# Moving the SBUF tiles of a fused attention and two-MLP kernel to multiples of 2048 bytes

## The chip, the core and the metric

The kernel runs on one core of a Trainium2 chip. The metric is the device time of one execution in microseconds (us); three runs of the kernel before gave 922.79, 922.91 and 923.17 us, a median of 922.91 us.

## What is computed

Attention over q, k, v of shape (4 batches, 8 heads, 576 positions, 64), where heads 0 to 3 see the last 32 positions and heads 4 to 7 every 32nd one; its output, 2304 tokens by 512, goes through two MLPs. In outline:

```
x = attention(q, k, v)                  # (2304, 512)
x = ((x @ w_a) * (x @ w_b)) @ w_out     # d_ff 1536
h = x @ w_in                            # d_ff 2048
out = (h * sigmoid(h)) @ w_out2         # (2304, 512)
```

The weights arrive as 8-byte floats, and the kernel makes 4-byte ones of them itself.

## The kernel before

**Matmuls.** A matmul to be precise to 4 bytes is done in three passes of the fp32r type: an operand is held as a pair (high part, rest), and `PASSES = ((0, 0), (0, 1), (1, 0))` names which part of the weights meets which part of the activations (line 733). Each pass is one LDWEIGHTS (128x128) and one MATMUL with a moving operand of up to 512 columns of 4 bytes, that is 2048 bytes in each partition. TensorE (PE) issues 3864 such matmuls in all, 3240 of them with 512 columns and 624, group 4's, with 256; the rest are the attention's small ones and 48 that keep the clock up.

**Order of the work.** Tokens are cut into four groups of 512 (0 to 3) and one of 256 (4). Batch 0's attention comes first, then groups 0 and 1 go through both MLPs one block at a time (lines 738, 1419 and 1439) with the attention of batches 1 to 3 laid between. After that an event list, sorted by planned time, sets the order for groups 2 to 4. Groups 2 and 3 share the up-projections: a block of both is computed in seven products instead of eight (`Chain`, line 1008 on; its matmul is line 1024), with sums and differences of the blocks as operands. Two chains at a time form a `twin`, whose places between products are filled with down-projections (`down`, line 1085). Twins run twice, once for the first MLP and once for the second; group 4 has its own blocks (lines 738 and 1211).

```
1024  nc.tensor.matmul(self.acc[acc], lhsT=w[:, wi, ...P columns], rhs=x[:, xi, c], ...)
 738  nc.tensor.matmul(ps[:, :T],     lhsT=w[:, wi, c*P:(c+1)*P],  rhs=x[:, xi, c, :T], ...)
1085  nc.tensor.matmul(accs[d],       lhsT=lhsT,                   rhs=rhs, ...)
```

**Operands of the seven products.** `CHAIN_ORDER = (1, 2, 6, 5, 7, 4, 3)`, twelve matmuls for each product of a twin. Products 1, 2 and 7 read A11, A12 and S3, which lie in tiles of the pool `xpool` (in the rows `x`); products 6, 5, 4 and 3 read S2, S1, A22 and S4, which lie in one tile `operands` (bytes 167872 to 200640 of each partition) of a pool `late`, opened on the right side of SBUF when attention has ended; all other operands of these matmuls lie below byte 138112. Their weights lie in tiles `w` (pool `wpool`), as everybody's do: ScalarE (ACT) writes the high part and VectorE (DVE) the rest (lines 730 and 731, 1314 and 1315), from pieces `raw` that a DMA has brought.

**Where tiles lie.** Pools are taken one behind the other from the left end of SBUF, and some from the right end. `xpool` holds activations x and y, `hpool` activations h in pairs, `tpool` and `epool` scratch, `rpool` and `kpool` the raw pieces and the 8-byte words (raw pieces take turns between the two), `spool` the small statistics of the softmax. In a partition, remainders of the start addresses by 2048 are, by the built program's memory plan (and in the last column for the changed program):

| tiles | before | changed |
|---|---|---|
| x, y (`xpool`), h (`hpool`), scratch (`tpool`) | 896 | 0 |
| weights' pairs w (`wpool`), raw pieces of `rpool` | 896 | 0 |
| words and raw pieces of `kpool`, scratch of `epool` | 1280 | 0 |
| `operands`, y2, u2, u3, p1, T of the pool `late` | 1984 | 0 |
| q and k tables, v of the attention | 1856, 960, 1984 | 1920, 1024, 0 |

A row of 512 columns is 2048 bytes, so every moving operand starts with its tile's remainder; a weight block of 128 columns starts 0, 512, 1024 or 1536 bytes behind it.

Of the kernel before, what the change touches and what calls it, by code (L numbers as in the profile page):

```python
# [9 lines left out]
F32 = mybir.dt.float32  # L10
# [8 lines left out]
P = 128  # L19
# [94 lines left out]
def attention_gated_mlp_silu_mlp(  # L114
# [32 lines left out]
    NG = len(groups)  # L147

    cpool = ctx.enter_context(tc.tile_pool(name="cpool", bufs=1))
    xpool = ctx.enter_context(tc.tile_pool(name="xpool", bufs=1))  # L150
    hpool = ctx.enter_context(tc.tile_pool(name="hpool", bufs=4))
    tpool = ctx.enter_context(tc.tile_pool(name="tpool", bufs=2))
    rpool = ctx.enter_context(tc.tile_pool(name="rpool", bufs=5))
    wpool = ctx.enter_context(tc.tile_pool(name="wpool", bufs=5))
    spool = ctx.enter_context(tc.tile_pool(name="spool", bufs=4))
    kpool = ctx.enter_context(tc.tile_pool(name="kpool", bufs=5))
    epool = ctx.enter_context(tc.tile_pool(name="epool", bufs=2))
    dpool = ctx.enter_context(tc.tile_pool(name="dpool", bufs=1, space=bass.MemoryType.DRAM))
    accp = ctx.enter_context(tc.tile_pool(name="accp", bufs=1, space=bass.MemoryType.PSUM))
    ringp = ctx.enter_context(tc.tile_pool(name="ringp", bufs=2, space=bass.MemoryType.PSUM))  # L160
    attp = ctx.enter_context(tc.tile_pool(name="attp", bufs=2, space=bass.MemoryType.PSUM))

    ppool = ctx.enter_context(tc.tile_pool(name="ppool", bufs=1, side="right"))
    ppool.tile([P, 8], F32, name="pad")
    att_ctx = ExitStack()
    lpool = att_ctx.enter_context(tc.tile_pool(name="lpool", bufs=1, side="right"))
    qpool = att_ctx.enter_context(tc.tile_pool(name="qpool", bufs=2, side="right"))
# [1 line left out]

    ident = cpool.tile([P, P], F32, name="ident")  # L170
    ident_b = cpool.tile([P, P], BF16, name="ident_b")
    mask_loc = apool.tile([P, 5, HALF], BF16, name="mask_loc", bufs=1)
    mask_str = apool.tile([P, JR], BF16, name="mask_str", bufs=1)

# [1326 lines left out]
```

## Time and profile before

| | |
|---|---|
| median of three runs | 922.91 us (922.79 to 923.17) |
| the profiled execution | 923.98 us, its span 922.2 us |
| busy: PE, its weight loads, DVE, ACT, POOL (GpSimd) | 98%, 79%, 70%, 58%, 10% of the span |
| granted TensorE clock, mean | 0.994 of 2.4 GHz |
| moved by DMA | 145.32 MB |

The profile counts an instruction as busy from its start to its end. A MATMUL's end lies some 0.16 us behind the start of the next, so how fast matmuls follow each other is read from where runs of them start, or from the chain of waits, which gives each piece only the time that it adds.

### The profile page before, as it was taken

The page shows a single profiled execution, that of the slowest core. Times are in us where ns is not written, and L with a number is a line of the kernel's source. Part 1 is how long each engine was busy: PE and PEld are TensorE (multiplying, and loading weights), DVE is VectorE, ACT ScalarE, POOL GpSimd, SP SyncE. Part 2 cuts the span into 40 slices and gives each one's busy share as a digit, 9 for nine tenths or more (in the row PEclk, how much of TensorE's full clock was granted, in tenths as well). Part 3 has the DMA queues.
Part 4 walks back from the last instruction along what each step waited for, and adds up shares of the span by engine and source line. Part 5 has one row for each costly group of instructions (what it writes and reads, how often), then busy time and mean ns, then how long its engine had stood idle before and what let it go on. Part 6 is the DMA issues. An engine that isn't in the chain of part 4 may idle for free.

```text
span 922.2 us, 16422 instructions
## 1 busy us (share of the span) xinstructions
PE 899.1 (98%) x5914; PEld 731.5 (79%) x5914; DVE 642.9 (70%) x1215; ACT 533.4 (58%) x1270; POOL 92.9 (10%) x162
## 2 busy tenths in 40 slices
PE   9799899999999999999999999999999999999998
PEld 5576677787778878778888888888999888878897
DVE  4577888776767867666677676656687766766475
ACT  4657788665677665564544444355575655554474
POOL 4532222011111010100000000000000000000000
PEclk9799999999999999999999999999999999999999
DMA  9999899898699993423332112233463121235471
GB/s 163 190 296 249 291 274 295 261 243 267 219 264 266 278 272 99 127 80 94 102 113 79 55 53 67 68 103 103 138 183 115 48 90 58 81 83 169 125 204 38
DMA packets 163697, 145.32 MB, mean 158 GB/s; under 512 B 96848, under 2 KB 119952, under 8 KB 163616
## 3 DMA queue, kind: packets, MB, share of 16 engines
q1 hardware_dynamic: 154758, 121.81, 49.6%
q0 software_dynamic: 6912, 21.66, 6.9%
q10 hardware_dynamic: 1946, 0.81, 0.5%
q8 instruction: 46, 0.75, 0.3%
q14 instruction: 35, 0.29, 0.1%
HBM read 121.70 MB, written 22.54 MB: 156 GB/s over the span
## 4 chain that ended last, share of the span: by engine, by line
PE 71%; DVE 9%; DMA 6%; ACT 6%; issue 4%; SPq 3%; POOL 0%; DVEq 0%; ACTq 0%; POOLq 0%
PE ring L738 16%; PE ring L1024 12%; PE att L1024 9%; PE acc L1085 8%; PE acc L1439 6%; PE acc L1211 4%; PE att L1085 4%; PE ring L1085 4%; PE acc L738 3%; PE acc L1419 3%; DMA words<-in_moe_w_b_dram 2%; ACT prs L501 2%; DVE w L731 2%; DVE raw L710 1%; ACT h L748 1%
## 5 line engine op out<-in xcount | busy, mean ns | idle before, releaser
L738 PE MATMUL ring<-x,w 128*128 128x512 f32 (+1 forms) x816 | 166.2, 356 | 4.6 <-DVE w L731 2.9
L738 PEld LDWEIGHTS ring<-x,w 128*128 128x128 f32 x816 | 132.3, 189 | 30.2 <-DVE w L731 7.4
L1315 DVE TENSOR_TENSOR w<-raw,w 128x512 fp32r<-128x512 f32 (+1 forms) x164 | 106.3, 656 | 28.9 <-ACT w L1314 26.2
L1314 ACT CAST w<-raw 128x512 fp32r<-128x512 f32 (+1 forms) x164 | 95.6, 592 | 20.4 <-PE att L1085 11.0
L731 DVE TENSOR_TENSOR w<-raw,w 128x512 fp32r<-128x512 f32 x136 | 93.2, 691 | 4.9 <-ACT w L730 4.4
L1439 PE MATMUL acc<-w,h 128*128 128x512 f32 x384 | 93.4, 392 | 1.3 <-DVE w L731 0.9
L738 PE MATMUL ring<-y,w 128*128 128x512 f32 x384 | 93.5, 392 | 0.3 <-DVE w L731 0.3
L1439 PEld LDWEIGHTS acc<-w,h 128*128 128x128 f32 x384 | 71.3, 188 | 17.7 <-DVE w L731 1.8
L738 PEld LDWEIGHTS ring<-y,w 128*128 128x128 f32 x384 | 71.3, 188 | 15.9 <-DVE w L731 0.7
L730 ACT CAST w<-raw 128x512 fp32r<-128x512 f32 x136 | 82.7, 620 | 2.0 <-PE acc L738 1.1
L1419 PE MATMUL acc<-h,w 128*128 128x512 f32 x288 | 72.5, 397 | 5.6 <-ACT w L730 2.5
L748 ACT CAST h<-h 128x512 fp32r<-128x512 f32 (+1 forms) x48 | 27.2, 567 | 83.0 <-DVE h L1060 40.7
L1419 PEld LDWEIGHTS acc<-h,w 128*128 128x128 f32 x288 | 52.7, 188 | 20.3 <-DVE w L731 4.8
L1024 PE MATMUL ring<-operands,w 128*128 128x512 f32 x240 | 60.6, 395 | 0.0
L749 DVE TENSOR_TENSOR h<-g,h 128x512 fp32r<-128x512 f32 (+1 forms) x64 | 39.9, 624 | 28.9 <-ACT h L748 28.9
L1024 PE MATMUL att<-operands,w 128*128 128x512 f32 x240 | 59.6, 393 | 0.0
L1024 PE MATMUL ring<-x,w 128*128 128x512 f32 x240 | 59.5, 391 | 0.0
L748 ACT CAST h<-g 128x512 fp32r<-128x512 f32 (+1 forms) x64 | 36.3, 567 | 37.7 <-DVE g L1411 30.2
L1130 POOL DMA_DIRECT2D out_dram<-o x16 | 8.7, 545 | 466.1 <-DVE o L1129 465.6
L501 ACT ACTIVATE prs<-sm,nm 128x54 f32<-128x54 f32 (+1 forms) x120 | 39.8, 333 | 25.1 <-DVE nm L486 25.1
L710 DVE SCALAR_TENSOR_TENSOR raw<-e,raw 128x512 int32<-128x512 int32 x68 | 49.0, 721 | 6.9 <-ACT e L687 0.9
L1024 PEld LDWEIGHTS ring<-operands,w 128*128 128x128 f32 x240 | 44.8, 188 | 11.4 <-DVE w L1315 1.3
(202 smaller groups left out, 1554.7 us busy)
## 6 DMA issues: line engine op xcount, KB each, us to landing
raw<-keptp SPq DMA_DIRECT2D x80, 256.0 KB
raw<-kepti SPq DMA_DIRECT2D x64, 256.0 KB
words<-in_moe_w_out_dram SPq DMA_DIRECT2D x28, 512.0 KB
raw<-kepto SPq DMA_DIRECT2D x48, 256.0 KB
raw<-kepta SPq DMA_DIRECT2D x36, 256.0 KB
raw<-keptb SPq DMA_DIRECT2D x36, 256.0 KB
words<-in_moe_w_in_dram SPq DMA_DIRECT2D x16, 512.0 KB
words<-in_moe_w_a_dram SPq DMA_DIRECT2D x12, 512.0 KB
```

Of the source, the lines that this page charges most:

```text
L501: nc.scalar.activation(out=place[s], in_=src[s], func=AF.Exp, bias=st["nm"][:, s:s + 1], scale=1.0, accum_out=su[:, s:s + 1],)
L710: nc.vector.scalar_tensor_tensor(out=z, in0=rebased.pop(c), scalar=3, in1=z, op0=ALU.logical_shift_left, op1=ALU.bitwise_or)
L730: nc.scalar.copy(out=o[:, 0], in_=t)
L731: nc.vector.tensor_tensor(out=o[:, 1], in0=t, in1=o[:, 0].bitcast(F32), op=ALU.subtract)
L738: nc.tensor.matmul(ps[:, :T], lhsT=w[:, wi, c * P:(c + 1) * P], rhs=x[:, xi, c, :T], start=(c == 0 and wi == 0 and xi == 0), stop=(c == CC ...
L748: nc.scalar.copy(out=o[:, 0, :T], in_=t32[:, :T])
L1024: nc.tensor.matmul(self.acc[acc], lhsT=w[:, wi, (2 * part + c) * P:(2 * part + c + 1) * P], rhs=x[:, xi, c], start=(begin and c == 0 and m ...
L1085: nc.tensor.matmul(accs[d], lhsT=lhsT, rhs=rhs, start=(first and wi == 0 and xi == 0), stop=(last and wi == 1))
L1314: nc.scalar.copy(out=o[:, 0, cols], in_=t)
L1315: nc.vector.tensor_tensor(out=o[:, 1, cols], in0=t, in1=o[:, 0, cols].bitcast(F32), op=ALU.subtract)
L1419: nc.tensor.matmul(accs[d], lhsT=w[:, wi, d * P:(d + 1) * P], rhs=h[:, xi], start=(j == 0 and wi == 0 and xi == 0), stop=(j == N1 - 1 and ...
L1439: nc.tensor.matmul(accs[t][:, :DM], lhsT=h[:, xi, t * P:(t + 1) * P], rhs=w[:, wi, :], start=(j == 0 and wi == 0 and xi == 0), stop=(j == ...
```

## The change

Two pads and one move. The unused tile that pads the right side grows from 8 to 504 floats; a new pool `lead` of 288 floats is put between the constants and `xpool`; the pool `spool` is opened behind `epool`. No computation, buffer count, transfer or order is edited: on each of the five queues the changed program has the same instructions in the same order with the same waits, and only addresses differ.

```diff
     cpool = ctx.enter_context(tc.tile_pool(name="cpool", bufs=1))
+    lead = ctx.enter_context(tc.tile_pool(name="lead", bufs=1))
     xpool = ctx.enter_context(tc.tile_pool(name="xpool", bufs=1))
...
     wpool = ctx.enter_context(tc.tile_pool(name="wpool", bufs=5))
-    spool = ctx.enter_context(tc.tile_pool(name="spool", bufs=4))
     kpool = ctx.enter_context(tc.tile_pool(name="kpool", bufs=5))
     epool = ctx.enter_context(tc.tile_pool(name="epool", bufs=2))
+    spool = ctx.enter_context(tc.tile_pool(name="spool", bufs=4))
...
     ppool = ctx.enter_context(tc.tile_pool(name="ppool", bufs=1, side="right"))
-    ppool.tile([P, 8], F32, name="pad")
+    ppool.tile([P, 504], F32, name="pad")
...
     ident_b = cpool.tile([P, P], BF16, name="ident_b")
+    lead.tile([P, 288], F32, name="lead")
```

## Rows read from the trace of the kernel before

**Rows 1.** The page's second part: busy tenths in 40 slices of the span.
```profile
PE   9799899999999999999999999999999999999998
DVE  4577888776767867666677676656687766766475
PEclk9799999999999999999999999999999999999999
DMA  9999899898699993423332112233463121235471
```
**Rows 2.** Stretches of the span: length, busy time of each engine (instructions), clock, DMA.
```profile
core 0: us, PE busy (x) PEld busy (x) DVE busy (x) ACT busy (x) POOL busy (x), PEclk, DMA share, GB/s
50.00:100.00 50.00, 46.27 (x385) 35.09 (x384) 37.68 (x80) 33.93 (x89) 15.18 (x25) 1.00 1.06 287
...
420.00:475.00 55.00, 55.00 (x244) 45.53 (x244) 39.63 (x67) 27.55 (x50) 0.05 (x1) 1.00 0.35 97
```
**Rows 3.** Chain of waits, a quiet stretch: start us, us added, engine and line, instructions.
```profile
424.51 2.72 PE ring L738 x12
427.23 2.72 PE acc L1439 x12
...
465.31 8.16 PE acc L1439 x36
```
**Rows 4.** Chain of waits, a stretch of the first MLP's twins.
```profile
489.95 2.75 PE att L1024 x12
492.70 2.77 PE ring L1024 x12
495.47 2.72 PE att L1024 x12
498.19 2.76 PE ring L1024 x12
500.95 2.75 PE att L1024 x12
```
**Rows 5.** Timeline of PE, the same stretch: start us, us, line, names, shapes, instructions.
```profile
489.79 2.91 PE L1024 MATMUL att<-operands,w 128*128 128x512 f32 x12
492.54 2.93 PE L1024 MATMUL ring<-x,w 128*128 128x512 f32 x12
495.31 2.88 PE L1024 MATMUL att<-x,w 128*128 128x512 f32 x12
498.03 2.93 PE L1024 MATMUL ring<-operands,w 128*128 128x512 f32 x12
500.79 2.91 PE L1024 MATMUL att<-operands,w 128*128 128x512 f32 x12
```
**Rows 6.** Stretches: the first MLP's twins, the second MLP's; columns as in rows 2.
```profile
473.31:612.05 138.74, 138.74 (x607) 113.76 (x606) 96.18 (x171) 57.56 (x109) 2.20 (x4) 1.00 0.24 73
...
707.77:821.05 113.28, 113.28 (x491) 91.62 (x490) 80.03 (x141) 60.30 (x116) 0.00 (x0) 1.00 0.23 71
```
**Rows 7.** Chain of waits, the second MLP's twins.
```profile
739.59 1.39 PE ring L1024 x6
740.98 0.70 PE acc L1085 x3
741.68 1.65 PE ring L1024 x6
```
**Rows 8.** Who waited for whom, 700 to 830 us: total us, times, longest.
```profile
PEld ring L1024 <- DVE w L1315: 1.3, 3, 0.4
```
**Rows 9.** Groups by shape, line 1024: instructions, busy us, mean ns, idle before.
```profile
L1024 PE MATMUL ring<-operands,w 128*128 128x512 f32 x240 | 60.6, 395 | 0.0
L1024 PE MATMUL att<-operands,w 128*128 128x512 f32 x240 | 59.6, 393 | 0.0
```
**Rows 10.** Groups by shape, ACT and DVE, splits of weights from two places.
```profile
L1314 ACT CAST w<-raw 128x512 fp32r<-128x512 f32 x144 | 88.6, 618 | 20.0 <-PE att L1085 11.0 <-ACT w L1314 5.3 <-PE ring L1024 1.1
L1314 ACT CAST w<-T 128x512 fp32r<-128x512 f32 x40 | 24.8, 619 | 17.7 <-DVE T L1324 16.9 <-PE acc L1439 0.8
...
L1315 DVE TENSOR_TENSOR w<-raw,w 128x512 fp32r<-128x512 f32 x144 | 98.7, 688 | 27.1 <-ACT w L1314 24.4
L1315 DVE TENSOR_TENSOR w<-T,w 128x512 fp32r<-128x512 f32 x40 | 27.0, 685 | 0.2
```
**Rows 11.** Stretches of 3.2 us that each hold one raw load; columns as in rows 2.
```profile
533.90:537.10 3.20, 3.20 (x16) 2.62 (x15) 1.67 (x3) 1.72 (x3) 0.00 (x0) 1.00 0.29 82
558.60:561.80 3.20, 3.20 (x16) 2.62 (x15) 1.65 (x3) 1.72 (x3) 0.00 (x0) 1.00 0.34 82
...
747.20:750.40 3.20, 3.20 (x16) 2.61 (x15) 0.73 (x2) 0.59 (x1) 0.00 (x0) 1.00 0.33 82
777.80:781.00 3.20, 3.20 (x16) 2.61 (x15) 0.73 (x2) 0.59 (x1) 0.00 (x0) 1.00 0.31 82
```
**Rows 12.** Chain of waits, first half: waits on kept pieces, runs behind a wait.
```profile
144.61 7.94 DMA raw<-kepta
...
301.90 5.48 DMA kepti<-raw
...
410.66 2.97 PE acc L1439 x12
```

## The prediction

> **What bounds the kernel now.** I read the busy slices first. PE is at nine tenths or more in 37 of 40 slices, at full clock after the second, and neither DVE nor DMA is up with it after the first third [rows 1]. So a change of the time must change how long PE needs, or the few waits it has. The stretches tell where these are: in 50 to 100 us PE is busy for 46.27 of 50.00 us beside a DMA share of 1.06, while from 420 us on it is busy without a hole (55.00 of 55.00) with DMA at a third [rows 2]. The late part can only get faster if matmuls follow each other faster.
>
> How fast they follow is in the chain of waits. In the quiet stretch every 12 fp32r matmuls add 2.72 us, and 36 add 8.16 us, 0.2267 us each [rows 3]. They read y, h and w there, all at remainder 896. In the twins the pieces aren't equal: 2.72 for one run of 12, but 2.75, 2.76 and 2.77 for others [rows 4]. The timeline names what each of them reads. The 2.75 and 2.76 are `operands`; the 2.77 is the first run on `x` behind an `operands` run; the 2.72 is the second run on `x`; the next `operands` run is slow again [rows 5]. The chain's pieces start 0.16 us behind the timeline's, since it counts from the end of what came before. So matmuls that stream `operands` take 2.75/12 = 0.229 us each, and a stream that comes behind them needs about one run to get back to its pace (2.77 - 2.72 = 0.05 us). PE waits for nobody in this (idle before: 0.0, for all 480 of them) [rows 9]. What is different about them is where they lie: `operands` starts at 1984 = 64 mod 128, while everything at 896, weights too, starts on a multiple of 128.
>
> **The change, part by part.**
>
> *x, y, h, w and `tpool` from 896 to 0.* All of them move by the same +1152 bytes, so a weight block and the row that streams through it keep their distance, which was already a multiple of 512. Pace now: 0.2267 us [rows 3]. I take it as unchanged. Bounds: a gain would need their start itself to cost something, a loss that the new one does; no row has an fp32r stream on a multiple of 256, so both are rivals below.
>
> *`operands` from 1984 to 0.* This is the only part that changes the distance of a matmul's two operands (from 64 to 0 mod 128). In the first MLP's twins, 138.74 us hold 606 started matmuls (607 with the one still draining from before) [rows 6]. At 0.2267 us they would take 606 x 0.22667 = 137.36 us; 1.4 us are lost. In the second MLP's twins, 113.28 us hold 489 (491 with two short ones still draining), which need 110.84 us; 2.4 us are lost [rows 6]. But of those, three waits stay: one run of 6 takes 1.65 us where its neighbour takes 1.39 [rows 7], and there are three in which PE's weight load waits for DVE's split (at most 0.4 us each, 1.3 in all, of which 0.26 lands on PE) [rows 7, 8]. 3 x 0.26 = 0.8 us, which leaves 1.6. Together 1.4 + 1.6 = 3.0 us. I take off 0.1 us for four short run-ins behind waits that remain, and say **2.9 us**. The lower end: only `operands`' own runs gain, 480 x (0.2296 - 0.2267) = 1.4 us, and the run-ins stay. The upper end: run-ins behind waits in the first half go as well. The chain has 12 runs of 12 that take 2.94 to 2.98 us behind a wait, the last at 410.66 [rows 12]; if each gave 0.05 to 0.08 us, that adds 0.9 us: 3.9 us.
>
> What is late next? Both stretches are covered by PE alone. DVE is busy for 96 of 139 and 80 of 113 us and ACT for less [rows 6], so 1% less of PE time doesn't make either the bound; their waits are on PE's results and come forward with it. What lies behind the twins, groups of 3 and 4, is PE's too, so I let the whole gain reach the end.
>
> *ACT and DVE.* Their operands move too. A split that reads T (1984) takes 619 ns on ACT and 685 on DVE; one that reads raw (896 or 1280) takes 618 and 688 [rows 10]. Nothing, in either direction; and DVE's is off PE's path but for the 0.8 us above.
>
> *DMA.* Raw pieces of `rpool` move from 896 (128 past a multiple of 256) to 0, those of `kpool` from 1280, a multiple of 256, to 0. Loads into `kpool` (533.90, 558.60) show shares of 0.29 and 0.34, loads into `rpool` (747.20, 777.80) 0.33 and 0.31 [rows 11]: means of 0.315 and 0.32, no difference. I take nothing. The Trainium skill, "DMA: Bandwidth & Descriptors", section "How a descriptor splits into AXI transactions", says that a piece not starting on a multiple of 256 bytes costs an extra transaction; for 2048 bytes at 128 past one that would be 68 beats instead of 64, an estimate from that page. By that rule a load into `rpool` would be some 6% longer, and the rows above don't show it. If 6% were true of stores and loads in the first half, it would shorten the waits on kept pieces in the chain, 7.94 and 5.48 us [rows 12], by 0.8 us, which lies inside the upper end.
>
> *Two pads, the place of `spool`.* No instruction; the statistics that move are 24 bytes long. Zero.
>
> **Sum.** The profiled execution took 923.98 us, 1.07 above the median of the runs. 923.98 - 2.9 = 921.1; the same step from the median gives 922.91 - 2.9 = **920.0 us**. About 0.2% (1.85 us) is what a measurement of this kernel tells from no change.
>
> **The rivals.**
>
> *Nothing happens (17%).* The slow runs may be due to the place of `operands`, at the top of the memory, not to the remainder of its start; it stays there. For it: this is the only operand tile above byte 138112, so place and remainder come together in every row. Against: the five w tiles, which stream in every second run of rows 3, reach from below byte 131072 to above it at one pace [rows 3], and the loss is a small constant for each matmul as from a bad start. Time: 922.9, less or more 0.4. The Trainium skill speaks for this rival: "SBUF — State Buffer", section "Who interferes with whom", gives PE two read ports of its own, one for the stream and one for the weights, that wait on nobody, and "Operand start alignment" asks for no more than the element's size. By these, 1984 is as good as 896 and the sum would be 0; the 2.75 against 2.72 in rows 4 speaks against it, but doesn't say which property of the address is at fault.
>
> *Slower (11%).* The starts at 896, 1408, 1920 and 384 (blocks of a tile at 896) are all 128 past a multiple of 256, and a stream on a multiple of 256 or 2048 was never seen. If that is a bad start for both of PE's reads, as 64 past one is now, all 512-column matmuls but the 480 run as `operands` do: 2760 x 0.0023 (0.2290 - 0.2267) = 6.4 us more, 929.3 us. It decides as soon as 2760 matmuls lose over 2.9/2760 = 1.1 ns each. Against: weight blocks start 0, 512, 1024 and 1536 bytes further and streams 2048, and a run of 12 goes through four blocks and several rows at one pace [rows 3], so steps of 512 and more don't matter; 128 and 256 are all that is left.
>
> *Everything gets faster (5%).* 512 columns in 0.2267 us are 0.0133 more than 512 / 2.4 GHz. If a part of it is due to starts off 256, up to 3240 x 0.0133 = 43 us could go; a tenth of it on top of the 2.9 gives 915.7 us. The Trainium skill, "TensorE: Matmul & The Clock Gate", Part 1, states 215.7 ns for back-to-back matmuls of 512 columns, measured in bf16, which would be 11 ns less than here; no fp32r row shows such a pace at any start.
>
> That the change doesn't do what it says I rule out: the memory plan of the changed program has every tile where the table says, and the instructions and waits are the same.
>
> **How the numbers follow.** Forecast 67%, own range 919.0 to 921.5. Of that I put 7 points at gains under 1.85 us (the lower end, 1.4). Faster: 60 + 5 = 65%. Same: 7 + 17 - 1 = 23%, the 1 being small losses of the second case. Slower: 11 + 1 = 12%. The range takes in the forecast, with 0.6 us beyond its own lower end for what the first half may add, and the case in which nothing happens: 918.4 to 923.3. It leaves out the last two (16%) and some edges.
>
> **What would show it.** Right: in the chain of waits, runs of 12 on `operands` add 2.72 us and the run on `x` behind them too; the first twins' 606 matmuls take about 137.4 us, the second's 489 about 111.7 with the three waits; the quiet stretch stays at 2.72. Wrong: `operands` still at 2.75 (place, not start); or the quiet stretch at 2.75 (the start at 0 is bad); or less waiting in the first half, which I don't count on; or the gain of the twins met by longer waits for DVE's splits.

## The result, and the profile after

| | before | changed |
|---|---|---|
| median of 4 runs | 922.85 us (922.49 to 923.17) | 915.04 us (913.94 to 916.83) |
| ratio | | 0.9917, 95% interval 0.9900 to 0.9934 |
| the profiled execution, its span | 923.98 us, 922.2 us | 914.96 us, 913.1 us |

The change gains 7.8 us where 2.9 were forecast; 915.0 lies below the range. Line numbers in the changed kernel are two higher: L1024 of [rows 4] is L1026, L738 is L740, L1439 is L1441, L1085 is L1087.

The page of the changed kernel, second part, the lines of [rows 1]:

```profile
PE   8799899999999999999999999999999999999998
DVE  4677887876767777666778667755687766766475
PEclk9999999999999999999999999999999999999999
DMA  9999899796899983333332221233463222235461
```

PE is still the busy one. Its clock has no dip in the second slice any more, and DMA falls to a third in the same slice as before, the sixteenth. The stretches of the changed kernel that answer to [rows 2, 6], the twins' ones moved to where they lie now:

```profile
50.00:100.00 50.00, 47.29 (x387) 35.36 (x386) 40.76 (x84) 35.29 (x90) 15.56 (x27) 1.00 0.99 302
...
420.00:475.00 55.00, 55.00 (x245) 45.53 (x244) 41.35 (x70) 28.04 (x51) 2.21 (x4) 1.00 0.38 111
466.55:603.90 137.35, 137.35 (x607) 113.74 (x606) 96.21 (x171) 57.68 (x109) 2.21 (x4) 1.00 0.24 73
699.58:811.97 112.39, 112.13 (x492) 91.32 (x490) 79.99 (x141) 60.39 (x116) 0.00 (x0) 1.00 0.23 71
```

The first twins take 137.35 us where they took 138.74, the second 112.39 where they took 113.28: 1.4 and 0.9 us. The larger part came before: the first twins start at 466.55 instead of 473.31, 6.8 us earlier. 6.8 + 1.4 + 0.9 = 9.1 us, the difference of the two spans. (Of the medians the difference is 7.8; the profiled execution of before lay 1.1 us above its median.) The chain of waits of the changed kernel, the lines of [rows 3, 4, 12] and two waits early on:

```profile
74.02 7.93 DMA words<-in_moe_w_a_dram
85.66 6.67 DMA words<-in_moe_w_out_dram
137.59 5.49 DMA raw<-kepta
...
458.56 8.16 PE acc L1441 x36
...
483.04 2.72 PE att L1026 x12
485.76 2.72 PE ring L1026 x12
488.48 2.72 PE att L1026 x12
491.20 2.72 PE ring L1026 x12
```

and the early waits in the chain of the kernel before:

```profile
75.31 5.55 DMA words<-in_moe_w_b_dram
82.74 8.71 DMA words<-in_moe_w_b_dram
92.65 6.55 DMA words<-in_moe_w_out_dram
```

In the quiet stretch 36 matmuls take 8.16 us as before, but the piece starts at 458.56 instead of 465.31. In the twins all runs of 12 take 2.72. Between 60 and 106 us the chain's long waits for words add up to 14.6 us instead of 20.8; one of 3.6 us for a load of q has come up beside them. What a timeline of PE in the changed kernel shows of two runs in the twins, to set beside [rows 5]:

```profile
482.87 2.88 PE L1026 MATMUL att<-operands,w 128*128 128x512 f32 x12
485.59 2.88 PE L1026 MATMUL ring<-x,w 128*128 128x512 f32 x12
```

and who waited for whom in 695 to 825 us, to set beside [rows 8]:

```profile
PEld ring L1026 <- DVE w L1317: 1.6, 3, 0.5
PEld ring L1026 <- ACT w L1316: 0.8, 3, 0.3
```

Runs on `operands` and on `x` now look alike. But the second MLP's twins wait more for the splits: 1.6 + 0.8 us of weight loads' waits instead of 1.3. The splits themselves take what they took (changed kernel, groups by shape, beside [rows 10]):

```profile
L1316 ACT CAST w<-T 128x512 fp32r<-128x512 f32 x40 | 24.8, 620 | 17.7 <-DVE T L1326 16.9 <-PE acc L1441 0.8
...
L1317 DVE TENSOR_TENSOR w<-T,w 128x512 fp32r<-128x512 f32 x40 | 27.0, 686 | 0.2
```

Where the 6.8 us come from is seen in the first stretches (columns as in [rows 2]). Before:

```profile
0.00:45.00 45.00, 37.89 (x536) 24.09 (x536) 21.28 (x71) 23.68 (x112) 23.41 (x44) 0.90 0.95 178
45.00:90.00 45.00, 42.31 (x424) 31.28 (x423) 33.02 (x72) 28.48 (x73) 12.98 (x22) 0.99 1.05 273
```

Changed:

```profile
0.00:45.00 45.00, 37.42 (x612) 24.21 (x613) 23.89 (x83) 25.83 (x123) 23.43 (x44) 1.00 0.93 195
45.00:90.00 45.00, 43.58 (x374) 33.25 (x373) 34.60 (x74) 31.26 (x78) 14.02 (x23) 1.00 1.00 303
```

DMA engines are busy all the time in both (shares 0.93 to 1.05), but move 195 and 303 GB/s instead of 178 and 273. The 200th fp32r matmul starts at 97.66 us instead of 104.51; the lead is there by then, and later stretches carry it on unchanged. By these rows and the long waits for words I take DMA as what bounds the first 100 us, and it moved more in the same time. Why it did is what the experiments ask.

### The profile page after: what moved, and what is told of

The parts are those of the page before. It is cut to its first block, busy times and chain, and to the rows that moved or that the text cites. A ratio compares the mean times of both kernels' runs of the same rounds, so it can differ in the third digit from the quotient of the medians.

```text
span 913.1 us, 16422 instructions
## 1 busy us (share of the span) xinstructions
PE 891.4 (98%) x5914; PEld 728.4 (80%) x5914; DVE 642.2 (70%) x1215; ACT 533.7 (58%) x1270; POOL 93.3 (10%) x162
## 4 chain that ended last, share of the span: by engine, by line
PE 68%; DVE 13%; ACT 8%; DMA 6%; issue 3%; SPq 2%; DVEq 0%; POOL 0%; ACTq 0%
PE ring L740 17%; PE ring L1026 11%; PE att L1026 7%; PE acc L1441 7%; PE acc L1087 6%; PE acc L1213 4%; PE att L1087 4%; PE ring L1087 4%; PE acc L1421 3%; PE acc L740 3%; ACT prs L503 2%; DVE w L733 2%; DMA words<-in_moe_w_a_dram 2%; DVE w L1317 1%; ACT h L750 1%
## 5 line engine op out<-in xcount | busy, mean ns | idle before, releaser
L740 PE MATMUL ring<-x,w 128*128 128x512 f32 (+1 forms) x816 | 166.2, 356 | 3.7 <-DVE w L733 2.2
L740 PEld LDWEIGHTS ring<-x,w 128*128 128x128 f32 x816 | 132.4, 189 | 29.3 <-DVE w L733 6.5
L1441 PE MATMUL acc<-w,h 128*128 128x512 f32 x384 | 93.5, 393 | 1.3 <-DVE w L733 0.9
L740 PE MATMUL ring<-y,w 128*128 128x512 f32 x384 | 93.5, 392 | 0.3 <-DVE w L733 0.3
L1441 PEld LDWEIGHTS acc<-w,h 128*128 128x128 f32 x384 | 71.3, 188 | 17.8 <-DVE w L733 1.7
L740 PEld LDWEIGHTS ring<-y,w 128*128 128x128 f32 x384 | 71.3, 188 | 15.9 <-DVE w L733 0.7
L1026 PE MATMUL ring<-operands,w 128*128 128x512 f32 x240 | 60.0, 392 | 0.3
L1026 PE MATMUL ring<-x,w 128*128 128x512 f32 x240 | 59.0, 389 | 0.0
L1026 PE MATMUL att<-operands,w 128*128 128x512 f32 x240 | 58.8, 389 | 0.0
L1026 PEld LDWEIGHTS ring<-operands,w 128*128 128x128 f32 x240 | 44.6, 188 | 11.3 <-DVE w L1317 1.6
```

What stands on the lines that cost most here:

```text
L740: nc.tensor.matmul(ps[:, :T], lhsT=w[:, wi, c * P:(c + 1) * P], rhs=x[:, xi, c, :T], start=(c == 0 and wi == 0 and xi == 0), stop=(c == CC ...
L1026: nc.tensor.matmul(self.acc[acc], lhsT=w[:, wi, (2 * part + c) * P:(2 * part + c + 1) * P], rhs=x[:, xi, c], start=(begin and c == 0 and m ...
L1441: nc.tensor.matmul(accs[t][:, :DM], lhsT=h[:, xi, t * P:(t + 1) * P], rhs=w[:, wi, :], start=(j == 0 and wi == 0 and xi == 0), stop=(j == ...
```

## The experiments

Two theories for the 6.8 us. **Clock**: the two dips to half speed, 1.2 GHz (before's profile, 28.9 to 35.8 and 42.6 to 46.0 us), went. **Pieces**: the attention's loads land in tiles that all began 192 past a multiple of 256 (`qld` and `kld`, which the loads of q and k fill, and `vl`, which those of v for heads 0 to 3 fill, at 960, 1472 and 1984), in pieces of 128 bytes (q, k) or 256 bytes (v); in the changed kernel they begin at 1024, 1536 and 0. And two for PE: **start** (each operand must begin on some multiple) and **distance** (from the weights' start to the stream's). `gap` and `lgap` are unused tiles that shift what follows them.

**The two sides apart.** r1_right has the right side of the change alone, r2_left the left alone.

```diff
--- before
+++ r1_right
-    ppool.tile([P, 8], F32, name="pad")
+    ppool.tile([P, 504], F32, name="pad")
--- changed
+++ r2_left
-    ppool.tile([P, 504], F32, name="pad")
+    ppool.tile([P, 8], F32, name="pad")
```

> Only the pad on the right side grows (8 to 504 floats): the chains' operands and the attention's tiles move to where the change puts them, x, h, w, raw and words stay at 896 and 1280. Theory 1 (two starts count: that of operands for PE, 2.9 us, and that of the attention's load tiles for the DMAs of the first half, some 5 us; the left side counts nothing): about 915, as the full change. Theory 2 (the left side's raw pieces, pairs and words shorten the DMAs): about 920, the operands' part alone. Theory 3 (what goes beyond 2.9 us is not a matter of addresses but of the runs): about 920.

> Only the left side moves (the pool lead, spool behind epool; x, h, w, raw, words at 0), operands stay at 1984 and the attention's tiles as before. Theory 1: 922.9, no change. Theory 2: about 918, all that goes beyond the operands' part. Theory 3: 922.9.

r1_right: 918.39 us, ratio 0.9957 (0.9944 to 0.9970). r2_left: 922.20, 0.9994 (0.9985 to 1.0002). So the right side, where `operands` and the attention's tiles lie, gave 4.6 us alone, and yet the first twins got longer in both: 139.12 and 139.27 us from the first start to the last, against 138.52 before and 137.13 in the changed kernel. The two sides don't add up: they work together on PE. Theory 1 had 915 for r1_right and Theory 2 had 918 for r2_left, and both missed; on Theory 3 these two runs don't decide. The chain of r2_left, in the twins:

```profile
487.35 2.80 PE att L1026 x12
490.15 2.74 PE ring L1026 x12
492.89 2.72 PE att L1026 x12
495.62 2.80 PE ring L1026 x12
```

`operands` stayed where it was, at 1984, and is slower than before (2.80 against 2.75), because the left side with w moved. That speaks for distance.

**Operands and the attention's tiles apart.** r3_ops puts `operands` at 0 and leaves the rest, the attention's tiles too; r4_att moves the attention's tiles alone.

```diff
--- before
+++ r3_ops
-    ppool.tile([P, 8], F32, name="pad")
+    ppool.tile([P, 504], F32, name="pad")
+    gpool = att_ctx.enter_context(tc.tile_pool(name="gpool", bufs=1, side="right"))
+    gpool.tile([P, 16], F32, name="gap")
--- before
+++ r4_att
+    gpool = att_ctx.enter_context(tc.tile_pool(name="gpool", bufs=1, side="right"))
+    gpool.tile([P, 496], F32, name="gap")
```

> The right pad of 504 floats, and a second one of 16 floats that goes with the attention's pools: operands at 0, the attention's tiles where they were before (load tiles 192 past a multiple of 256), the left side as before. Theory 1: 920.0, operands' runs of 12 at 2.72 us, and the first half as before (twins begin at about 473 us). Theories 2 and 3: about 920 as well.

> The right pad stays at 8 floats and a second one of 496 goes with the attention's pools: operands at 1984 as before, the attention's tiles where the change puts them (load tiles on multiples of 256), the left side as before. Theory 1: about 918, operands' runs of 12 still at 2.75 us, DMA packets of 128 bytes shorter on the mean and the twins beginning at about 467 instead of 473 us. Theories 2 and 3: 922.9.

r3_ops: 923.95, 1.0006 (0.9993 to 1.0019): no gain, where all three theories had about 920. Its chain in the twins:

```profile
489.65 2.80 PE att L1026 x12
492.45 2.73 PE ring L1026 x12
495.18 2.72 PE att L1026 x12
497.90 2.79 PE ring L1026 x12
```

`operands` at 0 beside w at 896 is slower than at 1984, though both starts are multiples of 128: the criterion of the forecast (multiples of 128, for the starts as for their distance) is not enough. r4_att: 917.64, 0.9946 (0.9934 to 0.9958), 5.3 us gained, where theories 2 and 3 had nothing, with PE's part untouched (its chain):

```profile
458.95 8.16 PE acc L1441 x36
...
483.59 2.75 PE att L1026 x12
486.34 2.77 PE ring L1026 x12
```

and its second stretch:

```profile
45.00:90.00 45.00, 44.43 (x417) 34.22 (x416) 37.33 (x84) 32.67 (x88) 13.63 (x22) 1.00 1.04 302
```

The start of the attention's tiles alone brings 302 GB/s and the quiet stretch at 458.95, nearly as early as in the changed kernel. It did so with a mean granted clock of 0.92 in the first 45 us, near before's 0.90. A kernel of the next part, s1_all896, gains 7.9 us with the clock as low as before's, 0.90 and 0.98 in its first two stretches against 0.90 and 0.99:

```profile
0.00:45.00 45.00, 38.67 (x563) 24.60 (x564) 21.88 (x72) 24.41 (x117) 23.20 (x44) 0.90 0.91 195
45.00:90.00 45.00, 44.44 (x414) 34.10 (x414) 36.38 (x80) 31.61 (x83) 13.76 (x22) 0.98 1.02 288
```

So the clock isn't the cause; the start of the attention's tiles is. Nor is it their place: in r3_ops, and in t4_match below, they lie 2048 bytes lower than before with the same remainders, and the quiet stretch begins at 464.93 and 464.01, with little or nothing of the lead. Whether it is the loads into these tiles, and which, is asked further down.

**Start or distance.** s1_all896 keeps the left side of before and puts `operands` at 896 too; t1_dist256 and s2_dist512 put it at 256 and 512 in the changed kernel. The gap keeps the attention's tiles where the changed kernel has them, by their remainders.

```diff
--- before
+++ s1_all896
-    ppool.tile([P, 8], F32, name="pad")
+    ppool.tile([P, 792], F32, name="pad")
+    gpool = att_ctx.enter_context(tc.tile_pool(name="gpool", bufs=1, side="right"))
+    gpool.tile([P, 224], F32, name="gap")
--- changed
+++ t1_dist256
-    ppool.tile([P, 504], F32, name="pad")
+    ppool.tile([P, 440], F32, name="pad")
...
+    gpool.tile([P, 64], F32, name="gap")
--- changed
+++ s2_dist512
-    ppool.tile([P, 504], F32, name="pad")
+    ppool.tile([P, 376], F32, name="pad")
...
+    gpool.tile([P, 128], F32, name="gap")
```

> The left side as before (x, h, w at 896), the attention's tiles as in the change (load tiles on multiples of 256), and the operands at 896 too, so that their distance to w is 0 as in the change but no start is a multiple of 2048. Theory 4 (the distance of operands and w by 512 sets PE's pace, not the start itself): operands' matmuls at 0.2267 to 0.2270 us, the first MLP's twins in 137.1 us, and about 2.3 us less than with the attention's tiles alone (917.6), so 915.3. Theory 5 (starts on a multiple of 2048, or of 256, are what is needed): operands' matmuls at 0.230 or more, twins 138.5 or more, 917.6 to 918.4.

> The full change with the operands 512 bytes up (512 past a multiple of 2048; a row of theirs now crosses such a multiple), the rest as in the change. Theory 4 by 512: operands' matmuls at 0.2267 to 0.2270 us as in the change, twins 137.1 us, 915. Theory 5, or a distance that counts by 2048: operands' matmuls slow, 0.229 to 0.233 us, twins 138.5 to 139.3, 916.5 to 918.

> The full change with the operands 256 bytes up, so 256 from w's blocks instead of 0. If the distance counts by 256 (or finer, which 128 has ruled out): operands' matmuls at 0.2267 to 0.2270 us, the first MLP's twins 137.1 us, about 915. If it counts by 512: operands' matmuls at 0.229 to 0.233 us, twins 138.5 to 139.3 us, 916.5 to 918.

s1_all896: 915.37, 0.9912 (0.9899 to 0.9925). s2_dist512: 914.35, 0.9911 (0.9897 to 0.9926). t1_dist256: 915.28, 0.9916 (0.9903 to 0.9929). All three gain what the change gains, and their first twins take 137.13 us as its do: Theory 4's numbers, not Theory 5's. The chain of s1_all896:

```profile
484.15 2.72 PE att L1026 x12
486.87 2.72 PE ring L1026 x12
489.59 2.72 PE att L1026 x12
```

and of t1_dist256:

```profile
483.54 2.72 PE att L1028 x12
486.26 2.72 PE ring L1028 x12
```

Not a single start of the matmuls in s1_all896's twins is a multiple of 256, and they have full pace. Put together, by `operands`' start less w's, modulo 256 (mean ns from one start to the next within `operands`' runs, and the chain's time for a run of 12):

| distance mod 256 | kernels | mean ns | 12 matmuls, us |
|---|---|---|---|
| 0 | changed, s1_all896, t1_dist256, s2_dist512 | 226.8 to 226.9 | 2.72 |
| 64 | before, r4_att | 230.4 | 2.75 |
| 128 | r1_right, r3_ops | 232.9 | 2.79 to 2.80 |
| 192 | r2_left | 233.4 | 2.80 |

Distance 0 was seen with both starts at 0 and with both at 128 past a multiple of 256; each other distance with one pair of remainders only (stream 192 and weights 128, 0 and 128, 192 and 0). That other pairs at the same distance take the same time is likely, but not shown.

Once the distance is 0, the left side's move (x, y, h, w and the raw pieces to 0) adds nothing that the medians show: without it 915.37, with it 915.04. About 1 us in the first half isn't excluded: r2_left's first twins got 0.75 us longer, and its median is 0.8 us lower all the same, its quiet stretch (one execution) at 462.62 instead of 465.31.

**Which pieces.** s3_qk moves q's and k's load tiles alone to a multiple of 256, t3_v v's alone. t2_qk128 puts q's and k's at 128 past one in the changed kernel. t4_match is the changed kernel with the attention's tiles back at 192 past: PE's part without the pieces.

```diff
--- before
+++ s3_qk
+    gpool.tile([P, 496], F32, name="gap")
...
+            lpool.tile([P, 16], F32, tag="lgap", name="lgap")
--- before
+++ t3_v
+    gpool.tile([P, 512], F32, name="gap")
...
+            lpool.tile([P, 48], F32, tag="lgap", name="lgap")
--- changed
+++ t2_qk128
+    gpool.tile([P, 32], F32, name="gap")
...
+            lpool.tile([P, 32], F32, tag="lgap", name="lgap")
--- changed
+++ t4_match
+    gpool.tile([P, 16], F32, name="gap")
```

> Only the load tiles of q and k (qld, kld; pieces of 128 bytes) on multiples of 256; v's tiles, the operands and the left side as before. Theory 6 (a DMA piece that crosses a multiple of 256 bytes of SBUF is dearer; both q and k and v count, by the packets' mean times 64512 x 1.9 ns against 23328 x 3.1 ns over 16 engines, 7.7 against 4.5 us): about 60% of the 5.3 us that all of the attention's tiles give, 919.7. If v's tiles do it alone: 923. If q and k do it alone: 917.6.

> Only the load tile of v of heads 0 to 3 (vl; pieces of 256 bytes) on a multiple of 256; q's and k's tiles cross as before, the operands and the left side as before. Theory 6: what the attention's tiles give together (5.3 us) less what q's and k's give alone (3.0): 920.7; packets of 128 bytes stay at 14.5 ns or more on the mean, those of 256 bytes get shorter. If q and k do it alone: 923.

> The full change with q's and k's load tiles at 128 past a multiple of 256 instead of 0 (v's tiles stay on one): no piece of 128 bytes crosses a multiple of 256, but every tile starts off one. Theory 6 (crossing): 915, packets of 128 bytes 13.1 to 13.5 ns on the mean as in the change. Theory 7 (the tile has to start on a multiple of 256): 918, packets of 128 bytes 14.5 ns or more.

> The full change, but the attention's tiles 64 bytes down, where they were before: left side and operands at 0, load tiles crossing multiples of 256. Theory 4 with 6: PE's part alone, twins 137.1 us in the first MLP and 115.3 in the second, the first half nearly as before: 920 to 921, near the 920.0 of the prediction. If the left side's raw pieces matter as well: 918 to 919.

In the table, the gain is against the median of the runs of before on the same chip (922.96, 923.28 or 923.31 us; for the changed kernel 922.85), the ratio is taken over all runs and so isn't the quotient of two medians, the quiet stretch is the start of its piece of 36 in the chain, and the last two columns are means over the trace's records of DMA packets, 64512 of 128 bytes and 23328 of 256:

| kernel | median, us | ratio (interval) | gain, us | quiet stretch, us | 128 B, ns | 256 B, ns |
|---|---|---|---|---|---|---|
| before | | | | 465.31 | 15.2 | 22.3 |
| t4_match | 920.16 | 0.9966 (0.9954 to 0.9979) | 3.2 | 464.01 | 14.3 | 21.8 |
| s3_qk | 920.27 | 0.9962 (0.9948 to 0.9975) | 3.0 | 459.54 | 13.5 | 19.7 |
| t3_v | 919.93 | 0.9970 (0.9961 to 0.9979) | 3.4 | 460.69 | 15.2 | 21.5 |
| r4_att | 917.64 | 0.9946 (0.9934 to 0.9958) | 5.3 | 458.95 | 13.5 | 19.2 |
| t2_qk128 | 915.16 | 0.9912 (0.9899 to 0.9925) | 8.2 | 457.32 | 13.2 | 19.0 |
| changed | 915.04 | 0.9917 (0.9900 to 0.9934) | 7.8 | 458.56 | 13.3 | 19.2 |

The last three columns are of one execution for each kernel, and these scatter: with the attention's tiles at before's remainders the means are 14.3 to 15.2 and 21.3 to 22.3 ns (before, r2_left, r3_ops, t4_match), and the profiled execution of s3_qk took 918.21 us, 2.1 below its median. So the gain of a kernel goes by the medians.

The second stretch of t4_match, against r4_att's 302 GB/s:

```profile
45.00:90.00 45.00, 43.62 (x406) 32.53 (x405) 33.81 (x74) 27.81 (x71) 13.55 (x22) 0.98 1.02 274
```

and its chain:

```profile
464.01 8.16 PE acc L1443 x36
...
480.33 2.72 PE att L1028 x12
```

t4_match has PE's part (2.72 on `operands`) and only 1.3 us of the early lead; r4_att has the lead and not PE's part. 5.3 + 3.2 = 8.5 us against 7.8, within the intervals (each some 1.1 us to either side). q's and k's load tiles alone gain 3.0 us, and t3_v, with `vl`, 3.4. The medians of packets are the same in all (13 and 18 ns): only a tail got shorter, in the changed kernel the 95th percentile of 128-byte packets from 28 to 13 ns and that of 256-byte ones from 46 to 27.

The tail isn't each tile's own. In s3_qk `vl` lies where it did, and the 256-byte packets still fell from 22.3 to 19.7; in t3_v `vl` was moved and they fell by 0.8 only, to 21.5, which is inside the scatter of kernels that left it in place. So q's and k's pieces delay the others beside them, and the shorter 256-byte packets that were expected of t3_v aren't shown. What gained 3.4 us in t3_v these means don't tell. Its second stretch does move as much as r4_att's, with the granted clock in the first as low as before's:

```profile
0.00:45.00 45.00, 38.74 (x564) 24.86 (x565) 21.50 (x72) 24.40 (x117) 23.37 (x44) 0.89 1.02 186
45.00:90.00 45.00, 44.45 (x417) 34.27 (x416) 36.30 (x79) 30.54 (x80) 13.54 (x22) 1.00 1.09 302
```

But t3_v isn't `vl` alone. Its gaps also shift the attention's other tiles, and by 256 these come to the remainders that they have in r4_att: t3_v is r4_att without q's and k's load tiles. (3.0 + 3.4 = 6.4 us against r4_att's 5.3 is within the intervals.) The attention's instructions on these tiles take no less time for it: a matmul on the q and k tables takes a mean of 219 ns (64 columns) in before, t3_v and r4_att alike. Which of the tiles brings the 3.4 us, and by what, stays open.

t2_qk128 loses nothing, so q's and k's tiles needn't begin on a multiple of 256. A piece of 128 bytes in a tile that begins 0 or 128 past such a multiple never lies across one, in a tile at 192 past every second piece does; that fits the rows of q and k, but a rule of multiples of 128 would fit them too, and no run tells these two apart.

**One more tile.** v's small tiles `vs` still begin at 96 in the changed kernel; s4_vs moves them to 0.

```diff
--- changed
+++ s4_vs
+    apool.tile([P, 24], F32, name="vgap", bufs=1)
```

> The full change, and the tile vs (v of heads 4 to 7, pieces of 256 bytes, at 96 past a multiple of 2048 in the change) moved to a multiple of 2048 by a gap of 24 floats. Theory 6: the pieces of vs no longer cross a multiple of 256, packets of 256 bytes get shorter on the mean, and the first half 0.5 to 2 us shorter: 913 to 914.5. If crossing doesn't matter: 915.0.

914.24 us, 0.9900 (0.9887 to 0.9914), the lowest median of all kernels. Packets of 256 bytes got shorter, as expected: 18.5 ns on the mean instead of 19.2, the 95th percentile 18 instead of 27. But the interval overlaps the change's (0.9900 to 0.9934), and the quiet stretch starts no earlier (458.77). Whether the kernel is faster for it stays open.

## Why the prediction was right or wrong

**PE's mechanism: right.** Runs on `operands`, and the first run on `x` behind them, went from 2.75 and 2.77 to 2.72; the first twins took 137.35 us where 137.4 was forecast; the quiet stretch stayed at 2.72. The forecast of 920.0 was a forecast of just this part, and t4_match, which has it without the rest, took 920.16 us. That fit is in part luck: the twins measured 1.4 + 0.9 = 2.3 us where the sum had 2.9, and in t4_match another 1.3 us had been gained before its quiet stretch, in the one execution profiled.

**The second twins: mis-sized.** The term was 1.6 us and measured 0.9. It took the three waits as given. When the runs between them got shorter, the weight loads waited 2.4 us for splits instead of 1.3, 1.1 us more. That is more than the missing 0.7, so part of it must have run beside PE's work. "The gain of the twins met by longer waits for DVE's splits" was named as a sign; the price was not in the sum.

**The criterion: wrong, with no effect on this sum.** The step said that `operands` was slow since it "starts at 1984 = 64 mod 128, while everything at 896 … starts on a multiple of 128". By r3_ops a stream at 0 beside weights at 896 is slower still, and by s1_all896 a pair at 896 is fast: it is the distance modulo 256. The prediction did name the distance, but by 128, and by that r3_ops has 0 and should have been fast. The change happens to make the distance 0 by 256 too, so the term came out by luck. The Trainium skill, "SBUF — State Buffer", section "Who interferes with whom", by which PE's stream and its weights have read ports that wait on nobody, doesn't agree with the four rows of the table by distance; the measurement decides. "Operand start alignment", which the prediction set beside it, says of itself that it is about what is legal and not about speed, so it was no support for that rival.

**The step that failed: "*DMA.* … I take nothing".** It compared raw pieces of 2048 bytes at 0 and 128 past a multiple of 256, found no difference (0.315 against 0.32, with shares from 0.29 to 0.34, too wide to see 6%), and from that priced all of DMA at nothing, with 0.8 us as a bound for the rule that speaks of 256 bytes. But the change's own table of starts ends with the attention: its q and k tables and v move by 64 bytes from remainders that are no multiples of 256, its load tiles with them, and those are filled in pieces of 128 and 256 bytes. They feed the one stretch that DMA bounds: [rows 2] show its share at 1.06 in 50 to 100 us, and I quoted that and didn't ask which transfers the change touches there. Measured: 5.3 us for the attention's tiles together (r4_att), 3.0 of them with q's and k's load tiles alone (s3_qk). The rule itself (the Trainium skill, "DMA: Bandwidth & Descriptors", section "How a descriptor splits into AXI transactions": a piece that doesn't start on a multiple of 256 bytes also pays for the unused bytes from the multiple below it; an extra transaction, as the prediction has it, follows for its 2048 bytes, not for every piece) agrees in direction for small pieces: 128-byte packets took a mean of 15.2 ns before and 13.3 after. For large ones it gives too much: of the 2048-byte packets behind 480 us, where every second raw load went to 128 past a multiple before and none did after, 78% took 84 ns before and 79% after, and under 1% took 85 to 92. The page counts bytes fetched, and here it is the place written to that moved, so the agreement is by result alone.

**The rivals.** *Nothing happens* and *Slower* fell: `operands` stayed at the top of the memory and got faster, and a stream on a multiple of 2048 runs at the same 2.72. *Everything gets faster* gave 915.7 us, close to the measured time, and is still wrong: no matmul in the quiet stretch got faster (8.16 us for 36, before and after). A time that fits says little about a mechanism; the row that it rests on does.

**The range** held PE's part with its bounds and nothing of DMA's but 0.8 us, so it ended 3.4 us above the median.

## What to carry to other kernels

When a change moves addresses, list every tile that it moves, its DMA pieces' size and its remainder, and look first at those that are loaded in the stretch that DMA bounds, not at the largest ones. Begin tiles that a DMA fills in pieces of 128 or 256 bytes on a multiple of 256, so that no piece lies across one; that was the fast place here, whichever rule is behind it. For fp32r matmuls, place streams and weights a multiple of 256 bytes apart: worth 1.6 to 2.9% of a matmul here (230.4 to 233.4 against 226.8 ns), so only where PE runs without holes.

## What the runs showed of the hardware that was not expected

The pace of 512-column fp32r matmuls depends on the distance of the two operands' starts modulo 256, in steps: 226.8, 230.4, 232.9 and 233.4 ns at 0, 64, 128 and 192; at distance 0 the start of the stream itself (0, 256, 512, 896) doesn't matter. A run that comes behind a slow one pays for it: the first run on `x` behind `operands` takes 2.77 us at distance 64, but 2.73 to 2.74 at 128 and 192, where `operands`' own runs are slower.

The DMA engines' busy share tells little of how much they move: in 45 to 90 us it was 1.05 with 273 GB/s before, 1.00 with 303 GB/s after, for the same list of transfers. And the tail of small packets is shared: in r4_att, where only the attention's tiles moved, 4096-byte packets into tiles that stayed took a mean of 187 ns instead of 201.
